# A longer list of first operations for local attention and channel mix on one core, with split products that follow it

## The chip, the cores and the metric

The kernel runs on one core of a Trainium2 chip. The core has a matrix engine (TensorE, PE in the profile), three engines for element-wise work (VectorE or DVE, ScalarE or ACT, GpSimd or POOL) and SyncE (SP), whose queue issues all the kernel's DMAs. The metric is the device time of one execution in microseconds; smaller is better.

## The reference

Two layers stand one behind the other. The first is chunked local attention on 4 batches, 8 heads, 768 tokens and 64 features a head; each chunk of 32 queries sees 16 keys to its left, its own 32, 8 to its right and 8 memory keys. The second is a channel mix over 512 features and 1024 hidden ones.

```python
for c in range(nc):                       # 24 chunks of 32 queries
    k_full = concat([mem_k, k[l_start:r_end]])
    v_full = concat([mem_v, v[l_start:r_end]])
    scores = scale * q_c @ k_full.T
    a = exp(scores - max(scores)); a = a / (sum(a) + 1e-9)
    out[c_start:c_end] = a @ v_full
...
x = out as (batch, token, 512)
x_prev = x shifted by one token, zeros first
xk = mu_k * x + (1 - mu_k) * x_prev
xr = mu_r * x + (1 - mu_r) * x_prev
v = maximum(xk @ w_k, 0) ** 2 @ w_v
return sigmoid(xr @ w_r) * v
```

The weights and mu come as 64-bit floats.

## The kernel before

The 3072 tokens are cut into 24 tiles of 128 (index t) and 12 units of two tiles (index u). The work is a list of some 770 named operations, each with a cost, the engines that may run it, its dependencies, and the buffers it takes and uses. The names are those of the prediction:

- **Weights.** There are ten chunks of 1 MiB: w0 and w1 hold w_r, w2 to w5 hold w_k, w6 to w9 hold w_v. Each is loaded as 64-bit words (`w4.load`) and turned into a pair of fp32r tiles by five steps: `mag` (ScalarE) and `low` (VectorE) take the word apart, `join` (VectorE) puts a 32-bit float together, `hi` rounds it (ScalarE or VectorE), and `lo` is the rest (VectorE or GpSimd).
- **Attention.** `qk` and `vw` are a tile's loads. For each unit `s` makes the scores on TensorE, `max` and `sub` (VectorE) and `exp` (ScalarE) the softmax, `sum` (one reduction and two small steps) and `norm` finish it. For each tile `t` transposes on TensorE, `bd.0` and `bd.1` copy the result into a block-diagonal tile, `a` multiplies with the values, and `x` copies the result into the unit's xT. For the first tile of a unit, `x` also copies one column from the unit before, always on ScalarE.
- **Mix.** `df` is the difference to the shifted tokens, `mix.1` and `mix.0` the two blends, and `xh` and `xl` their high and low halves. `mix.1`, `xh.1`, `xl.1` feed the gate and `mix.0`, `xh.0`, `xl.0` the hidden layer.
- **Products.** A product of two pairs is three fp32r products. `g` is the gate (tile pr, 128x512 matmuls), `h` the hidden layer (tile ph, 128x256 matmuls), `v` the output (tile pv, 128x512). `relu`, `sq`, `kh` and `kl` turn a hidden bank into a pair, `sig` is the gate's sigmoid, `o` multiplies, and `out` stores. In unit 0, `h0.n` takes one w_k chunk (w2 + n) for all four hidden banks, so that it can begin before all chunks are there; `g0.n` and `v0.n` do the same with w_r and w_v. `g0.0` needs w0, h0.0 needs w2. In later units `h` and `g` are one bank each.

Buffers tie the loads to the work. Weight words and qk tiles share four buffers (`big`), vw has three. SyncE's queue goes in order, and a load waits there until the buffer's last reader is done.

The order is fixed in Python before anything is issued. `Plan.order` first places the items of the string FIRST, in that order, each on the engine written behind the @. What is left it places by itself, always the operation that can start first by the plan's costs; the order of TensorE alone then follows due times made from `te_order`. Each engine runs its own operations in the order in which they were placed; only semaphores tie the engines together. Between TensorE's operations ahead of h0.0 the kernel puts warm-up matmuls on zeros wherever the plan sees a gap. Each of these is two instructions in the trace.

`product` can write its 512 columns in two matmuls of 256. Before, that is so for the last product of `g` in the second tile of each unit and of `v` in the second tile of unit 1.

Of the kernel before, what the change touches and what calls it, by code (L numbers as in the profile page):

```python
# [16 lines left out]
P = 128  # L17
# [7 lines left out]
KT = DM // P  # L25
# [7 lines left out]
QPU = UTOK // P  # L33
# [5 lines left out]
TABLE = 1.3  # L39
BLOCK = 2.75  # L40
FIRST = """
w4.load@dma w4.low@dve qk1@dma w4.mag@act w4.join@dve w4.hi@dve w4.lo@dve qk0@dma s0@pe max0@dve sub0@dve
w3.load@dma w3.mag@act w3.low@dve w3.join@dve exp0@act sum0@dve norm0@dve qk3@dma w3.hi@act w3.lo@pool qk2@dma
s1@pe max1@dve id@dma t0@pe bd0.0@act bd0.1@act mu@dma t1@pe sub1@dve w2.load@dma w2.low@dve w2.mag@act
w2.join@dve exp1@act sum1@dve bd1.1@act vw1@dma bd1.0@act vw0@dma a0@pe a1@pe x0@act x1@act norm1@dve t2@pe
bd2.1@act bd2.0@act qk5@dma df0@dve mix0.1@dve mix0.0@dve w5.load@dma w5.mag@act w2.hi@act w2.lo@dve vw2@dma
qk4@dma s2@pe max2@dve xh0.0@act xl0.0@pool t3@pe bd3.1@act sub2@dve vw3@dma bd3.0@act w1.load@dma w1.mag@act
a2@pe a3@pe w5.low@dve w5.join@dve w5.hi@act w0.load@dma w0.mag@act w1.low@dve w1.join@dve w0.low@dve
w0.join@dve qk6@dma w5.lo@dve exp2@act sum2@dve norm2@dve w0.hi@act w0.lo@dve xh0.1@act xl0.1@dve x2@act
x3@act df1@dve w1.hi@act w1.lo@dve h0.0@pe h0.1@pe h0.2@pe h0.3@pe relu0.1@act sq0.1@act relu0.0@act kh0.1@dve  # L50
kl0.1@dve sq0.0@act kh0.0@act t4@pe bd4.1@act bd4.0@act t5@pe bd5.0@act bd5.1@act qk7@dma s3@pe max3@dve
g0.0@pe g0.1@pe mix1.1@dve xh1.1@dve xl1.1@dve vw4@dma a4@pe kl0.0@dve w7.load@dma w7.low@dve w7.mag@act
mix1.0@dve xh1.0@dve xl1.0@dve w6.load@dma w6.mag@act w6.low@dve vw5@dma a5@pe relu0.2@act sq0.2@act
relu0.3@act sq0.3@act kh0.3@act w7.join@dve w7.hi@dve sig0.0@act sig0.1@act kh0.2@act vw6@dma w8.load@dma
w8.mag@act g1.0@pe sig1.0@act w7.lo@dve w6.join@dve w6.hi@dve w6.lo@dve g1.1@pe sig1.1@act kl0.3@dve vw7@dma
kl0.2@dve h1.0@pe h1.1@pe h1.2@pe h1.3@pe relu1.0@dve sq1.0@act qk9@dma x4@act x5@act sub3@dve exp3@act
relu1.1@dve
"""
PE_COST = {"s": 1.4, "t": 0.45, "a": 1.05, "g": BLOCK, "h": BLOCK, "v": BLOCK}
BIAS = {"act": 0.0, "dve": 0.3, "pool": 0.3}  # L60
# [22 lines left out]
class Plan:  # L83
# [123 lines left out]
def local_attention__then__channel_mix(  # L207
# [31 lines left out]
    def ps(tag, name, n=1):  # L239
        return psA.tile([P, n * 512], F32, tag=tag, name=name, bufs=bufs[tag])  # L240
# [22 lines left out]
    plan = Plan(bufs)  # L263
# [9 lines left out]
    def either(**alts):  # L273
        return [(n, *alts[n]) for n in alts]
# [60 lines left out]
    def wdeps(hl, ks):  # L335
        return [o for k in ks for o in wdone[id(hl[0]), k]]
# [181 lines left out]
    def channel_mix(u):  # L518
        b, t0 = units[u]

        def hilo(m):
            return T["xh", u, m], T["xl", u, m]

        def product(p, x, w, start, stop, halves):
            step = DM // 2 if halves else DM
            for a in range(0, DM, step):
                nc.tensor.matmul(  # L527
                    p[:, a : a + step], x, w[:, a : a + step], start=start, stop=stop and a + step == DM
                )

        def gate(c, ks):
            p = T["pr", u, c]
            xh, xl = hilo(1)
            for k in ks:
                wh, wl = (w[k // 2][:, k % 2 * DM : (k % 2 + 1) * DM] for w in wr_hl)
                for n, (x, w) in enumerate(((xh, wh), (xh, wl), (xl, wh))):
                    stop = k == KT - 1 and n == 2
                    product(p, x[:, k, c * P : (c + 1) * P], w, k + n == 0, stop, stop and c == QPU - 1)

        def hidden(f, ks):  # L540
            p = T["ph", u, f]
# [8 lines left out]
                        stop = k == KT - 1 and n == 2 and (u > 0 or i == 1)  # L550
                        nc.tensor.matmul(z, w, x[:, k], start=start, stop=stop)  # L551
# [18 lines left out]
        first = u == 0  # L570
# [42 lines left out]
        for n in range(FT // 2):  # L613
# [10 lines left out]
            w = wdeps(wk_hl, [n] if first else range(KT))  # L624
# [8 lines left out]
        ks = []  # L633
        for f in range(FT // 2):
# [28 lines left out]
            o2 = op(f"kh{u}.{f}", either(act=(0.6,), dve=(0.36, True)), f_hi, [ob], new=[kh], use=[kf])  # L663
# [49 lines left out]
    for u in range(NU):  # L713
        channel_mix(u)
    engines = {"act": nc.scalar, "dve": nc.vector, "pool": nc.gpsimd}
    warm = None
    zero = zero_sb.bitcast(F32)
    zeros = zero.unsqueeze(1).to_broadcast([P, 4, P])
    busy = 0.0
    with tc.manual_schedule():  # L720
        for o in plan.order(FIRST.split()):
            if o.eng == "pe":
                n = 0 if ("ph", 0, 0) in T else int((o.start - busy - 0.1) / (0.86 if busy else 1.72))
                for _ in range(n):
                    warm = warm or ps("m", "warm")
                    nc.tensor.matmul(warm, zero, zeros, start=True, stop=True)  # L726
# [50 lines left out]
```

## Time and profile before

| | |
|---|---|
| median of 3 runs | 418.64 us (417.03 to 419.3) |
| the profiled execution, its own time | 414.7 us |
| its span, first to last instruction | 412.9 us |
| TensorE busy | 402.4 us, 97% of the span |
| VectorE, ScalarE, GpSimd busy | 247.0, 193.5 and 17.7 us |
| read from HBM, written | 42.01 MB, 6.29 MB |

The views name an instruction by its line, its engine, the operation and what it writes and reads (out<-in), without buffer numbers. In the timeline the first number is the start and the second the length, in us from the span's start; what ended the engine's idle time stands in brackets. In the groups by line the numbers after the bar are the busy time, the mean length of one in ns, and the idle time ahead. A busy TensorE isn't one at its peak, since its instructions overlap and their ends are modelled. VectorE is 92% to 100% busy between 40 and 90 us; from 90 us on the kernel repeats one unit's work about every 32 us.

### The profile page before, as it was taken

To read this page: it belongs to the slowest core of one execution; us is meant where nothing else is said; L and a number is where in the kernel's file an instruction comes from. 1 tells how busy PE (TensorE), PEld (TensorE's weight loads), DVE (VectorE), ACT (ScalarE), POOL (GpSimd) and SP (SyncE) were. 2 spreads that over 40 slices of the span, in tenths; PEclk is the share of its full clock that TensorE was granted. 3 is DMA by queue.
4 is the path that set the end of the run, shared out by engine and by line. 5 is a ranking of instruction groups with operands and counts; after the bars stand their busy time and mean duration, and the time that the engine had idled before them with its cause. 6 is when DMAs were issued, how large, how long until landed. Compare 5 with 4: busy or idle time off the path is not lost.

```text
span 412.9 us, 9915 instructions
## 1 busy us (share of the span) xinstructions
PE 402.4 (97%) x4463; PEld 349.7 (85%) x4463; DVE 247.0 (60%) x356; ACT 193.5 (47%) x275; POOL 17.7 (4%) x20
## 2 busy tenths in 40 slices
PE   7789999999999999999999999999999999999996
PEld 3448989888988988988988988988988998998994
DVE  3999999981286287178169169169259348337021
ACT  2376964840633634543553453463363264363250
POOL 2202000010000010010010010010010010010000
PEclk9999999999999999999999999999999999999999
DMA  8998966211261062062053043034003002000001
GB/s 324 375 415 313 397 210 223 76 51 52 78 249 59 0 233 79 0 214 94 2 193 115 2 160 148 2 144 139 27 2 129 25 3 78 25 2 27 25 2 51
DMA packets 12906, 48.94 MB, mean 119 GB/s; under 512 B 1472, under 2 KB 1600, under 8 KB 12352
## 3 DMA queue, kind: packets, MB, share of 16 engines
q1 hardware_dynamic: 12864, 48.31, 32.0%
q8 instruction: 35, 0.57, 0.6%
q14 instruction: 7, 0.06, 0.0%
HBM read 42.01 MB, written 6.29 MB: 117 GB/s over the span
## 4 chain that ended last, share of the span: by engine, by line
PE 92%; DMA 5%; DVE 2%; SPq 0%; issue 0%; DVEq 0%
PE pv L527 33%; PE ph L551 32%; PE pr L527 16%; PE px L444 5%; DMA qk<-in_qk_dram 5%; PE s L365 4%; PE pt L427 2%; DVE mx L378 0%; DVE mag L318 0%; DVE e L382 0%; DVE sum L394 0%; PE warm L726 0%; SPq L295 0%; DVE o L696 0%; DVE raw L314 0%
## 5 line engine op out<-in xcount | busy, mean ns | idle before, releaser
L551 PE MATMUL ph<-xh,wkh 128*128 128x256 f32 x384 | 106.2, 277 | 0.0
L551 PE MATMUL ph<-xl,wkh 128*128 128x256 f32 x384 | 106.1, 276 | 0.0
L551 PE MATMUL ph<-xh,wkl 128*128 128x256 f32 x384 | 106.0, 276 | 0.0
L655 DVE TENSOR_TENSOR kl<-kf,kh 128x512 fp32r<-128x512 f32 x47 | 32.3, 690 | 112.3 <-ACT kh L269 112.2
L527 PE MATMUL pv<-wvh,kh 128*128 128x512 f32 x192 | 76.8, 400 | 0.0
L527 PE MATMUL pv<-wvh,kl 128*128 128x512 f32 (+1 forms) x193 | 75.0, 389 | 0.0
L527 PE MATMUL pv<-wvl,kh 128*128 128x512 f32 x192 | 74.8, 390 | 0.0
L551 PEld LDWEIGHTS ph<-xh,wkh 128*128 128x128 f32 x384 | 72.1, 188 | 0.1
L551 PEld LDWEIGHTS ph<-xl,wkh 128*128 128x128 f32 x384 | 72.1, 188 | 0.0
L551 PEld LDWEIGHTS ph<-xh,wkl 128*128 128x128 f32 x384 | 72.1, 188 | 0.0
L638 ACT ACTIVATE kf<-ph 128x512 f32<-128x512 f32 x46 | 27.5, 599 | 56.8 <-PE ph L551 53.0
L527 PEld LDWEIGHTS pv<-wvh,kh 128*128 128x128 f32 x192 | 36.0, 188 | 8.2
L527 PEld LDWEIGHTS pv<-wvh,kl 128*128 128x128 f32 x193 | 36.2, 188 | 7.8
L527 PEld LDWEIGHTS pv<-wvl,kh 128*128 128x128 f32 x192 | 36.1, 188 | 6.9
L527 PE MATMUL pr<-wrh,xh 128*128 128x512 f32 x96 | 37.6, 391 | 0.0
L527 PE MATMUL pr<-wrh,xl 128*128 128x512 f32 (+1 forms) x108 | 37.5, 365 | 0.0
L527 PE MATMUL pr<-wrl,xh 128*128 128x512 f32 x96 | 37.4, 389 | 0.0
L598 ACT ACTIVATE sg<-pr 128x512 f32<-128x512 f32 x24 | 14.1, 598 | 47.8 <-PE pr L527 47.7
L269 ACT CAST kh<-kf 128x512 fp32r<-128x512 f32 x46 | 28.5, 620 | 4.2 <-POOL kf L647 2.4
L444 PEld LDWEIGHTS px<-aTz,vw 128*64 128x64 f32 x768 | 23.6, 138 | 7.0 <-issue 5.7
L269 ACT CAST xh<-xf 128x1024 fp32r<-128x1024 f32 x11 | 11.6, 1053 | 38.0 <-DVE xf L500 38.0
L645 ACT ACTIVATE kf<-kf 128x512 f32<-128x512 f32 x38 | 24.0, 632 | 7.2 <-DVE kf L640 6.0
(62 smaller groups left out, 498.9 us busy)
## 6 DMA issues: line engine op xcount, KB each, us to landing
qk<-in_qk_dram SPq DMA_DIRECT2D x24, 768.0 KB, 5.9
vw<-in_vw_dram SPq DMA_DIRECT2D x24, 512.0 KB, 5.5
out_dram<-o SPq DMA_DIRECT2D x24, 256.0 KB, 2.0
raw<-in_w_k_dram SPq DMA_DIRECT2D x4, 1024.0 KB, 8.7
raw<-in_w_v_dram SPq DMA_DIRECT2D x4, 1024.0 KB, 7.3
raw<-in_w_r_dram SPq DMA_DIRECT2D x2, 1024.0 KB, 7.8
id_sb<-in_ident_dram SPq DMA_DIRECT2D x1, 64.0 KB, 6.4
mu_sb<-in_mu_dram SPq DMA_DIRECT2D x1, 4.0 KB, 6.1
```

The costliest lines, as they stand in the source:

```text
L269: e.copy(dst, src)
L365: nc.tensor.matmul(s5[CHUNK * j : CHUNK * (j + 1), h, c, r, :], q4[z, r, j, :], k4[z, r, j, :], start=True, stop=True,)
L427: nc.tensor.transpose(p[:, n * P : (n + 1) * P], e[:, n // 2, c, n % 2, :], id_sb)
L444: nc.tensor.matmul(p3[64 * h : 64 * h + 64, 2 * g : 2 * g + 2, CHUNK * j : CHUNK * j + CHUNK], v[:, g, h, j, :], a[:, h, g, j, :], start=True,
L527: nc.tensor.matmul(p[:, a : a + step], x, w[:, a : a + step], start=start, stop=stop and a + step == DM)
L551: nc.tensor.matmul(z, w, x[:, k], start=start, stop=stop)
L598: nc.scalar.activation(T["sg", u][:, c * DM : (c + 1) * DM], T["pr", u, c], AF.Sigmoid)
L638: e.activation(r, T["ph", u, f], AF.Relu)
L645: e.activation(q, q, AF.Square)
L655: e.tensor_sub(l, T["kf", u, f], T["kh", u, f].bitcast(F32))
```

## The change

FIRST grows from 170 to 273 items, and all are new in order: it now reaches up to unit 2's output products (v2.3), where the old list ended in unit 1's hidden layer. The weight chunks come in another order (w5, w2, w3, w4, w0, w1, w7, w6, w9, w8 in place of w4, w3, w2, w5, w1, w0, w7, w6, w8, w9). On TensorE h0.0 has the same eleven operations ahead of it as before, and behind it the first units are arranged anew; from h3.0 on the order is that of before. Where the first output product v0.0 came behind all of unit 1's hidden products, it now comes ahead of h1.3.

The second part: which last products are written in two matmuls is no longer fixed by tile and unit. The kernel looks through TensorE's order for each `h` that directly follows a `g` or `v`, and marks the latter.

```diff
-w4.load@dma w4.low@dve qk1@dma w4.mag@act w4.join@dve w4.hi@dve w4.lo@dve qk0@dma s0@pe max0@dve sub0@dve
...
+w5.load@dma w5.mag@act w5.low@dve w5.join@dve w5.hi@act w5.lo@dve qk0@dma qk1@dma s0@pe max0@dve id@dma w2.load@dma
...
-        def gate(c, ks):
+        def gate(c, ks, kick):
...
-                    product(p, x[:, k, c * P : (c + 1) * P], w, k + n == 0, stop, stop and c == QPU - 1)
+                    product(p, x[:, k, c * P : (c + 1) * P], w, k + n == 0, stop, stop and c in kick)
...
-        def value(c, fs):
+        def value(c, fs, kick):
...
-                        product(p, x[:, tc_], w, f + n == 0, stop, stop and c == QPU - 1 and u == 1)
+                        product(p, x[:, tc_], w, f + n == 0, stop, stop and c in kick)
...
-                        gate(c, range(n * KT // 2, (n + 1) * KT // 2))
+                        gate(c, range(n * KT // 2, (n + 1) * KT // 2), ())
...
-                    gate(n, range(KT))
+                    gate(n, range(KT), [n] if ("g", u, n) in kicks else ())
...
-                    value(c, fs)
+                    value(c, fs, [QPU - 1 if first else c] if ("v", u, n) in kicks else ())
...
+    done = plan.order(FIRST.split())
+    te = [o.name for o in done if o.eng == "pe"]
+    kicks = set()
+    for a, b in zip(te, te[1:]):
+        if b[0] == "h" and a[0] in "gv":
+            kicks.add((a[0], *map(int, a[1:].split("."))))
...
-        for o in plan.order(FIRST.split()):
+        for o in done:
```

ScalarE, from the copy of a1's result to what follows xh0.0, before. The names end in a number that the program gives each tile; mag5 is chunk w5, aTz0 and aTz1 are the block-diagonal tiles, wkh0 is w2's high half, xh0_0 the hidden layer's high half of unit 0.

```order
L269 COPY xT0_344<-px1_327 128x4x128
L269 COPY aTz0_86<-pt2_350 64x16x32 x2
L311 ACTIVATE mag5_372<-raw5_370 128x1024
L269 CAST wkh0_66<-mag2_294 128x1024
L269 CAST xh0_0_450<-df0_359 128x1024
L269 COPY aTz1_87<-pt3_454 64x16x32 x2
```

The same stretch of ScalarE after:

```order
L276 CAST wkh1_67<-mag3_203 128x1024
L318 ACTIVATE mag4_433<-raw4_431 128x1024
L276 COPY aTz0_86<-pt2_420 64x16x32 x2
L276 COPY aTz1_87<-pt3_440 64x16x32 x2
L465 COPY xT1_473<-xT0_324 128x4
L276 COPY xT1_473<-px2_456 128x4x128
L276 CAST xh0_0_494<-df0_350 128x1024
L276 COPY xT1_473<-px3_476 128x4x128
L276 CAST wkh2_68<-mag4_433 128x1024
L276 CAST xh0_1_609<-xf0_425 128x1024
```

Both tiles' copies (bd) and x2 (the two rows that write xT1) have moved ahead of xh0.0, w4.mag stands ahead of them, and w4.hi and the gate's xh0.1 follow closely.

VectorE between sub2 and norm2 before (norm2 is the last row; wkl3 is w5's low half):

```order
L382 TENSOR_TENSOR e2_460<-s2_382,mx2_448 128x1024
L314 TENSOR_SCALAR raw5_370<-raw5_370 128x1024
L318 SCALAR_TENSOR_TENSOR mag5_372<-mag5_372,raw5_370 128x1024
L314 TENSOR_SCALAR raw1_465<-raw1_465 128x1024
L318 SCALAR_TENSOR_TENSOR mag1_467<-mag1_467,raw1_465 128x1024
L314 TENSOR_SCALAR raw0_507<-raw0_507 128x1024
L318 SCALAR_TENSOR_TENSOR mag0_509<-mag0_509,raw0_507 128x1024
L324 TENSOR_TENSOR wkl3_73<-mag5_372,wkh3_69 128x1024
L394 TENSOR_REDUCE sum2_519<-e2_460 128x16
L395 TENSOR_SCALAR sum2_519<-sum2_519 128x16
L396 RECIPROCAL sum2_519<-sum2_519 128x16
L400 TENSOR_TENSOR e2_460<-e2_460,sum2_519 128x1024
```

VectorE from xl0.0 on after (wkl1 and wkl2 are the low halves of w3 and w4, wrl0 and wrl1 of w0 and w1); sum2's two small steps and norm2 come next:

```order
L517 TENSOR_TENSOR xl0_0_496<-df0_350,xh0_0_494 128x1024
L321 TENSOR_SCALAR raw0_452<-raw0_452 128x1024
L331 TENSOR_TENSOR wkl1_71<-mag3_203,wkh1_67 128x1024
L331 TENSOR_TENSOR wkl2_72<-mag4_433,wkh2_68 128x1024
L383 MEMSET s2_352 32x2x4x8
L385 TENSOR_REDUCE mx2_614<-s2_352 128x16
L389 TENSOR_TENSOR e2_620<-s2_352,mx2_614 128x1024
L325 SCALAR_TENSOR_TENSOR mag0_611<-mag0_611,raw0_452 128x1024
L321 TENSOR_SCALAR raw1_616<-raw1_616 128x1024
L325 SCALAR_TENSOR_TENSOR mag1_618<-mag1_618,raw1_616 128x1024
L331 TENSOR_TENSOR wrl0_84<-mag0_611,wrh0_82 128x1024
L331 TENSOR_TENSOR wrl1_85<-mag1_618,wrh1_83 128x1024
```

xl0.0, which was GpSimd's, is VectorE's now, and four low halves stand ahead of norm2 in place of one.

GpSimd's first element-wise operations after (before they were w3's low half, xl0.0, one kl of unit 1, and then one square in each unit):

```order
L331 TENSOR_TENSOR wkl0_70<-mag2_185,wkh0_66 128x1024
L517 TENSOR_TENSOR xl0_1_624<-xf0_425,xh0_1_609 128x1024
L662 TENSOR_TENSOR kl0_1_758<-kf0_1_635,kh0_1_729 128x512
L662 TENSOR_TENSOR kl0_0_768<-kf0_0_637,kh0_0_732 128x512
L662 TENSOR_TENSOR kl0_2_1023<-kf0_2_816,kh0_2_917 128x512
L662 TENSOR_TENSOR kl0_3_1070<-kf0_3_901,kh0_3_961 128x512
L662 TENSOR_TENSOR kl1_2_1224<-kf1_2_1211,kh1_2_1216 128x512
L662 TENSOR_TENSOR kl2_1_1404<-kf2_1_1309,kh2_1_1399 128x512
```

On TensorE, h0.0 to h0.3, t4, t5, s3, g0.0, g0.1, a4, a5, g1.0 before has become h0.0 to h0.3, s3, g0.0, t4, t5, g0.1, a4, a5, s4, g1.0.

More of the change, by code (lines that the diff above doesn't have):

```diff
@@ L41 @@
 FIRST = """
-w4.load@dma w4.low@dve qk1@dma w4.mag@act w4.join@dve w4.hi@dve w4.lo@dve qk0@dma s0@pe max0@dve sub0@dve
[L43 to L56, printed above, removed]
@@ L57 @@
-relu1.1@dve
+w5.load@dma w5.mag@act w5.low@dve w5.join@dve w5.hi@act w5.lo@dve qk0@dma qk1@dma s0@pe max0@dve id@dma w2.load@dma
+w2.mag@act w2.low@dve qk3@dma qk2@dma sub0@dve w2.join@dve exp0@act w2.hi@act sum0@dve w3.load@dma w3.mag@act vw0@dma
+s1@pe norm0@dve t0@pe t1@pe w3.low@dve w2.lo@pool qk4@dma bd0.1@act bd0.0@act bd1.0@act a0@pe bd1.1@act vw1@dma
+max1@dve sub1@dve qk5@dma exp1@act x0@act w3.join@dve sum1@dve a1@pe x1@act df0@dve s2@pe norm1@dve mu@dma t2@pe
+mix0.1@dve w3.hi@act w4.load@dma w4.mag@act vw2@dma w4.low@dve bd2.0@act bd2.1@act t3@pe bd3.1@act vw3@dma mix0.0@dve
@@ new lines @@
+w0.load@dma bd3.0@act a2@pe x2@act a3@pe w4.join@dve xh0.0@act xl0.0@dve h0.0@pe w0.low@dve w3.lo@dve x3@act h0.1@pe
+w4.hi@act w4.lo@dve vw4@dma vw5@dma h0.2@pe h0.3@pe xh0.1@act w0.mag@act max2@dve w1.load@dma w1.mag@act sub2@dve
+qk7@dma xl0.1@pool w0.join@dve exp2@act w1.low@dve w1.join@dve w0.hi@act w0.lo@dve vw6@dma w1.hi@act relu0.1@act
+relu0.0@act qk6@dma sq0.0@act s3@pe g0.0@pe qk9@dma w1.lo@dve sum2@dve sq0.1@act kh0.1@act norm2@dve kh0.0@act
+w7.load@dma w7.mag@act t4@pe t5@pe bd4.0@act bd4.1@act qk8@dma df1@dve bd5.0@act max3@dve kl0.1@pool mix1.1@dve
@@ new lines @@
+sub3@dve bd5.1@act kl0.0@pool g0.1@pe a4@pe a5@pe relu0.2@act xh1.1@act s4@pe sq0.2@act xl1.1@dve g1.0@pe relu0.3@act
+exp3@act mix1.0@dve sq0.3@act x4@act x5@act sum3@dve kh0.2@dve xh1.0@act g1.1@pe w6.load@dma w6.mag@act norm3@dve
+t6@pe t7@pe xl1.0@dve w6.low@dve w7.low@dve w7.join@dve sig0.0@act vw7@dma sig0.1@act vw8@dma kh0.3@act bd6.1@act
+h1.0@pe h1.1@pe w9.load@dma max4@dve sub4@dve sig1.0@act sig1.1@act kl0.2@pool bd6.0@act a6@pe h1.2@pe bd7.1@act
+bd7.0@act kl0.3@pool w6.join@dve relu1.0@act sq1.0@act w6.hi@dve w8.load@dma a7@pe w9.mag@act w8.mag@act w9.low@dve
@@ new lines @@
+w7.hi@act w8.low@dve w6.lo@dve w9.join@dve relu1.1@act v0.0@pe h1.3@pe w9.hi@act w8.join@dve x6@act sq1.1@act qk13@dma
+vw9@dma w7.lo@dve df2@dve w8.hi@act w8.lo@dve x7@act qk10@dma qk11@dma v0.1@pe v0.2@pe mix2.1@dve mix2.0@dve w9.lo@dve
+vw10@dma kh1.0@act exp4@act kl1.0@dve xh2.0@act xl2.0@dve relu1.2@act sq1.2@act kh1.1@dve kh1.2@act kl1.1@dve
+relu1.3@act qk12@dma kl1.2@pool v0.3@pe o0.1@dve h2.0@pe o0.0@dve h2.1@pe out0.1@dma sq1.3@dve xh2.1@act kh1.3@dve
+kl1.3@dve relu2.0@act xl2.1@dve sq2.0@dve out0.0@dma df3@dve relu2.1@act mix3.1@dve mix3.0@dve v1.0@pe v1.1@pe v1.2@pe
@@ L58 @@
+sq2.1@act v1.3@pe o1.0@dve h2.2@pe kh2.1@dve o1.1@dve out1.1@dma kl2.1@pool kh2.0@act kl2.0@dve relu2.2@dve sq2.2@act
+h2.3@pe relu2.3@act kh2.2@dve sq2.3@act kl2.2@dve out1.0@dma g2.0@pe sig2.0@act g2.1@pe xh3.1@act kh2.3@dve v2.0@pe
+kl2.3@dve v2.1@pe v2.2@pe o2.0@dve sig2.1@act v2.3@pe
 """
```

## The prediction

> **What bounds the kernel now.** I read the page first, its busy times (the share of the span in brackets):
>
> ```profile
> PE 402.4 (97%) x4463; PEld 349.7 (85%) x4463; DVE 247.0 (60%) x356; ACT 193.5 (47%) x275; POOL 17.7 (4%) x20
> ```
>
> TensorE is the bound. The chain of waits in order of time (start, length, what) says where it still has room:
>
> ```profile
> 1.64 7.77 DMA qk<-in_qk_dram
> ...
> 18.82 11.87 DMA qk<-in_qk_dram
> ...
> 36.02 11.10 PE ph L551 x96
> 47.11 0.87 PE pt L427 x8
> 47.99 1.41 PE s L365 x89
> 49.40 5.69 PE pr L527 x25
> 55.08 2.02 PE px L444 x64
> 57.10 5.67 PE pr L527 x25
> 62.77 10.90 PE ph L551 x96
> ...
> 409.09 0.69 DVE o L696
> ```
>
> From 36.02 (h0.0, behind a3) to 409.09 every piece is TensorE's own work, one behind the other. That work (373.07 us) is the same in both kernels, and so are the 3.8 us behind it. So the time can change in two ways only: **h0.0 starts at another moment than 36.0, or TensorE waits behind it**. A new order cannot gain more than it takes off those 36 us, and both lists put the same eleven items (s0 to s2, t0 to t3, a0 to a3) ahead of h0.0.
>
> **Front: when can h0.0 start?** These are the timeline rows of ScalarE, TensorE, VectorE and GpSimd there (start, length):
>
> ```profile
> 17.32 3.00 DVE L400 TENSOR_TENSOR e<-e,sum 128x1024 f32<-128x1024 f32 x1
> 25.49 0.20 ACT L456 COPY xT<-zero_sb 128x4 f32<-128x4 f32 x1
> 25.59 0.58 ACT L269 COPY xT<-px 128x512 f32<-128x512 f32 x1
> 25.69 1.15 PE L444 MATMUL px<-aTz,vw 128*64 128x64 f32 x32
> 26.88 0.59 ACT L269 COPY xT<-px 128x512 f32<-128x512 f32 x1 [0.71 <-PE px L444]
> 27.75 0.63 PE L427 MATMUL pt<-id_sb,e 128*128 128x128 f32 x4
> 28.21 1.88 PE L726 MATMUL warm<-zero_sb 128*128 128x512 f32 x4
> 28.47 1.17 ACT L269 COPY aTz<-pt 64x512 f32<-64x512 f32 x2 [1.01 <-PE pt L427]
> 29.55 1.14 ACT L311 ACTIVATE mag<-raw 128x1024 f32<-128x1024 f32 x1
> 30.36 1.67 DVE L500 SCALAR_TENSOR_TENSOR df<-df,mu_sb,xT 128x256 f32<-128x256 f32 x4
> 32.06 1.05 ACT L269 CAST xh<-df 128x1024 fp32r<-128x1024 f32 x1 [0.43 <-DVE df L500]
> 33.18 2.40 POOL L510 TENSOR_TENSOR xl<-df,xh 128x1024 fp32r<-128x1024 f32 x1 [13.95 <-ACT xh L269]
> ```
>
> Before, mix0.0 ends at 32.03, xh0.0 follows at once and xl0.0 takes 2.40 us on GpSimd, to 35.58. After, xl0.0 is VectorE's: the like-sized L324 takes 1.22 (row below), 1.2 saved. But xh0.0 now stands on ScalarE behind w4.mag, bd2.0 to bd3.0 and x2, hence behind a2. VectorE reaches mix0.0 no earlier: norm0 ends some 0.3 sooner than 20.32, and one more "low" (0.69) stands ahead of mix0.0, so it ends near 32.3. norm1 ends near 28.2 (20.0 plus low, max, sub, join, sum, df, norm, 8.5 us, less 0.1 for each overlap), t2 follows, and the first copy comes 0.72 behind t2 (27.75 to 28.47): 29.0.
>
> ScalarE runs w4.mag ahead of these copies, so **the landing of w4 decides**. Ahead of and with w4 the new queue has four weight chunks of 1 MiB, six qk of 0.75 and two vw of 0.5: 9.5 MiB. The second qk lands at 1.64 + 7.77 = 9.41 with 2.5 MiB done, in both orders, leaving 7.0 MiB. Two rates can be had:
>
> ```profile
> 20.00:30.00 10.00, 8.47 (x86) 4.88 (x86) 9.65 (x14) 7.13 (x12) 0.00 (x0) 1.00 1.02 417
> ```
>
> At 417 GB/s (2.51 us a MiB) w4 lands at 27.0. But qk4 landed at 18.82 + 11.87 = 30.69 with 10 MiB done, 7.5 MiB in 21.28 us or 2.84 a MiB, and by that w4 lands at 29.3. Late end: w4.mag to 30.45, two copies (1.17) to 31.65, a2, x2 1.19 later (25.69 to 26.88) to 33.55, xh0.0 to 34.6, xl0.0 to 35.85, h0.0 at 35.9. TensorE's own side says the same: a3 at 32.85, then four warm-up matmuls (1.88) up to 35.85. Early end: copies from 29.0, a2 at 30.25, x2 to 32.1, xh0.0 from 32.3, h0.0 at 34.65. The gain on the front is so 0.1 to 1.3 us. I take 0.4, nearer the late end, whose rate was measured over the same stretch.
>
> **Behind h0.0: the wait at t4.** Before, norm2 ended at 45.7 and t4 ran at 47.11, after the four hidden products. After, s3 and g0.0 come first, so t4 is due 11.10 + 1.41 + 5.69 / 2 = 15.4 us behind h0.0's start, and norm2 needs more of VectorE than before, since w3.lo, w4.lo and both w_r chunks' joins and lows now stand ahead of it. The durations:
>
> ```profile
> L314 DVE TENSOR_SCALAR raw<-raw 128x1024 uint32<-128x1024 uint32 x10 | 6.9, 689 | 4.7 <-DMA raw<-in_w_k_dram 4.7
> L318 DVE SCALAR_TENSOR_TENSOR mag<-mag,raw 128x1024 uint32<-128x1024 uint32 x10 | 12.2, 1223 | 1.0 <-ACT mag L311 0.5
> L324 DVE TENSOR_TENSOR wkl<-mag,wkh 128x1024 fp32r<-128x1024 f32 x3 | 3.7, 1221 | 0.0
> L378 DVE TENSOR_REDUCE mx<-s 128x16 f32<-128x1024 f32 x12 | 14.7, 1224 | 0.4
> L382 DVE TENSOR_TENSOR e<-s,mx 128x1024 f32<-128x1024 f32 x12 | 14.6, 1219 | 0.2
> L394 DVE TENSOR_REDUCE sum<-e 128x16 f32<-128x1024 f32 x12 | 14.5, 1210 | 0.0
> 44.48 1.23 DVE L400 TENSOR_TENSOR e<-e,sum 128x1024 f32<-128x1024 f32 x1
> 45.62 1.22 DVE L324 TENSOR_TENSOR wrl<-mag,wrh 128x1024 fp32r<-128x1024 f32 x1
> ```
>
> From xl0.0's end: two lows 1.38, two joins 2.45, four lo 4.88, max2 with its memset 1.4, sub2 1.2, sum2 with two small steps 1.7, norm2 1.23: 14.2 us, less 0.09 for each of some seven that start before the one ahead has ended (44.48 + 1.23 against 45.62), 13.6 us. That would be 1.8 ahead of need. What undoes it is GpSimd:
>
> ```profile
> 16.89 2.35 POOL L324 TENSOR_TENSOR wkl<-mag,wkh 128x1024 fp32r<-128x1024 f32 x1 [13.94 <-ACT wkh L269]
> L655 POOL TENSOR_TENSOR kl<-kf,kh 128x512 fp32r<-128x512 f32 x1 | 1.3, 1293 | 52.3 <-ACT kh L269 52.3
> ```
>
> While the first ran, norm0 took 3.00 instead of 1.23: it ended 1.08 after GpSimd had done (19.24, 20.32). So a VectorE operation on two SBUF tiles stands still until GpSimd is through. The new order gives GpSimd xl0.1 when xh0.1 is done: ScalarE's x3 (0.59), w4.hi and xh0.1 (1.05 each) follow xh0.0, which ends 1.25 ahead of h0.0, so 1.4 behind h0.0. That falls inside w3.lo, and w4.lo is next on VectorE. If GpSimd (2.4 us) comes in ahead of it, w4.lo ends near 4.9 instead of 3.0 behind h0.0: 1.9 lost, and the cover is gone. Then norm2 is ready at about 14.3, just as GpSimd gets kl0.1 (five ScalarE steps on 512 columns, 0.58 each like x0's copy or a little more, behind the hidden products' end at 11.1: 14.0 to 14.4): another 1.29 or nothing. If nothing, df1 stands still instead, and sub3 gates s4: behind norm2 come df1, max3, mix1.1 and sub3 (5.2 us of VectorE) against t4, t5, g0.1, a4, a5 (5.6 of TensorE), so the wait only moves to s4 and shrinks by 0.4. **I take 1.3 us; the bounds are 0 (GpSimd never first) and 2.7 (kl0.0 follows kl0.1 at once, another 1.3).**
>
> The Trainium skill, "SBUF — State Buffer", section "Who interferes with whom", speaks against this change: GpSimd and VectorE share a port pair, the one that issues first holds it for its whole instruction, and a VectorE operation with two SBUF inputs is blocked by a GpSimd operation that reads SBUF. The trace agrees (norm0, 3.00). By that rule the sum is +0.9; without it, -0.4.
>
> **The rest.** Split products: eleven instead of thirteen last products are halved.
>
> ```profile
> 62.15 0.39 PE L527 MATMUL pr<-wrl,xh 128*128 128x512 f32 x1
> 62.38 0.40 PE L527 MATMUL pr<-wrh,xl 128*128 128x256 f32 x2
> L551 PEld LDWEIGHTS ph<-xh,wkh 128*128 128x128 f32 x384 | 72.1, 188 | 0.1
> ```
>
> Two halves took 0.40 together, one whole 0.39: nothing. But v0.0 to h1.3 is now a boundary from 512 to 256 columns without a split, which before never has. If hidden products then ran at the load's 188 ns instead of 114 (10.90 / 96), 24 of them would cost 1.8; below, nothing is to be had. I take 0: h0.0 behind a3 has no split either and pays 0.2 in all. Later moves cost nothing: v0.0, the first to need w_v, still has unit 1's gate and most of its hidden layer ahead of it, some 40 us of TensorE behind h0.0's start, and now s4 and t6 to a7 too; from h3.0 on TensorE's order is that of before.
>
> **Sum**, against the profiled execution (span 412.9, its own time 414.7): -0.4 + 1.3 + 0 = **+0.9, span 413.8**. The median of the runs shown, 418.64, lies 3.9 above that execution; the change is added to it: 419.5.
>
> **Rivals.**
> - *VectorE keeps its port* (30%): w4.lo issues before GpSimd's xl0.1, norm2 is done 1.8 ahead of need, nothing waits at t4, only the front's gain is left: 418.2, down to 417.3 with w4 landing early. For: it follows w3.lo without a gap. Against: in the one case of the trace GpSimd was first. The skill's rule in that section, that who issues first wins, allows both.
> - *GpSimd takes it twice* (15%): kl0.0 goes directly behind kl0.1 while norm2 stands; wait 2.6, front 0.1: 421.1, slower. It decides if kh0.0 is done before kl0.1's 1.29 us are over, which it should be as ScalarE's next step, and if the waiting VectorE doesn't come between.
> - *The split does not act where it is needed* (7%): v0.0 isn't the last step of its sum, so the flag set for it halves nothing; with 1.8 on top of the forecast: 421.3.
> - *The front gains more than its early end* (3%): the whole 1.3 and more, with no wait behind: 416.5 or less.
> - Forecast, the wait eats the front's gain (45%): 419.5, by itself 418.4 to 420.5.
>
> **How the numbers follow.** All but the two slower rivals and the last one stay within 0.5% (2.1 us, about what a measurement can tell from no change). Faster by more needs the last rival: 0.05. Slower by more: both slower rivals lie at +2.5 and +2.7, some of them below the bound: 0.18. The rest, 0.77, is within. The range goes from the early end with no wait (417.3), less half a microsecond for the runs' own spread (417.03 to 419.3), to the slow rivals (421.3) with the same: 416.8 to 421.8.
>
> **What would show it.** In the chain of waits: h0.0's first ph piece at 35.5 (34.65 to 35.9), behind xl0.0 on VectorE. A w4.lo of some 3 us beside GpSimd's xl0.1, norm2 stretched beside kl0.1, and a VectorE piece of 1 to 1.5 us between pr and pt at about 51. If w4.lo and norm2 both take 1.22, the rival holds. h1.3's 24 matmuls should take 2.73, 4.5 if the split matters. I am wrong if h0.0 starts before 34.5, or if a wait of over 0.5 us stands behind s4.

## The result, and the profile after

| | before | after |
|---|---|---|
| median (four runs each) | 418.40 us (417.03 to 419.30) | 422.90 us (422.67 to 423.12) |
| span of the profiled execution | 412.9 us | 421.1 us |
| first hidden product h0.0 starts | 35.95 us | 40.31 us |
| from there to the end of the span | 377.0 us | 380.8 us |

The ratio after to before is 1.011, with a 95% interval of 1.0082 to 1.0139: slower by some 4.5 us, and above the predicted range, which ended at 421.8. The page of after gives TensorE 404.5 us of busy time and before 402.4, nearly the same. The time went into pauses and into a slower clock. First the head of the page, TensorE's busy share and its granted clock, in 40 slices of 10.5 us, the clock in tenths:

```profile
span 421.1 us, 9904 instructions
PE   8749989999999999999999999999999999999996
PEclk9997999999999999999999999999999999999999
```

The third slice of PE and the fourth of PEclk stand out: around 26 to 37 us TensorE pauses, and then runs at a lower clock. The chain of waits of after (start, length, what) names the pieces there:

```profile
25.48 1.49 PE s L372 x104
26.96 4.57 issue
31.54 0.43 PE s L372 x4
31.96 2.00 PE warm L739 x2
33.97 1.71 PE pt L434 x8
```

"issue" is time in which the engine waited for nothing that the profile shows. It lies in the middle of s2: 124 of its 128 small matmuls run in 1.56 us, TensorE stands for 4.57 us, and four more follow. No load, no buffer and no other engine is named. Then two warm-up matmuls and the eight transposes t2 and t3 take 2.00 and 1.71 us; four and eight took 1.88 and 0.87 in before's profile. The windows of after say why (PE busy, PEld, DVE, ACT, POOL, then the granted clock, the DMA share and GB/s):

```profile
28.00:30.00 2.00, 0.00 (x0) 0.00 (x0) 2.00 (x6) 1.14 (x1) 0.00 (x0) 0.89 1.03 408
34.00:36.00 2.00, 2.00 (x9) 1.80 (x8) 0.00 (x0) 1.07 (x3) 0.00 (x0) 0.50 0.08 23
```

The clock is at a half from 30 to 36 us. By the mean of 0.89 between 28 and 30 us it fell at about 29.6 (0.44 us at a half), some 2.6 us into the pause. The Trainium skill, "TensorE: Matmul & The Clock Gate", section "What's actually happening", has the clock at half after at least one idle window of about 3.4 us. Here it fell sooner, and the measurement decides.

Behind h0.0, the two waits in which VectorE and GpSimd meet. Timeline rows of VectorE and GpSimd, and the two rows of TensorE that waited (in brackets the idle time and what ended it):

```profile
41.38 4.56 DVE L331 TENSOR_TENSOR wkl<-mag,wkh 128x1024 fp32r<-128x1024 f32 x2
42.06 2.79 POOL L517 TENSOR_TENSOR xl<-xf,xh 128x1024 fp32r<-128x1024 f32 x1 [23.46 <-ACT xh L276]
55.78 3.51 POOL L662 TENSOR_TENSOR kl<-kf,kh 128x512 fp32r<-128x512 f32 x2 [10.92 <-ACT kh L276]
55.80 2.34 DVE L407 TENSOR_TENSOR e<-e,sum 128x1024 f32<-128x1024 f32 x1
58.06 2.31 DVE L499 TENSOR_TENSOR df<-xT 128x1024 f32<-128x1024 f32 x1
58.19 1.09 PE L434 MATMUL pt<-id_sb,e 128*128 128x128 f32 x8 [1.75 <-DVE e L407]
64.64 1.74 PE L372 MATMUL s<-qk 64*32 64x64 f32 x128 [0.58 <-DVE e L389]
```

w3.lo and w4.lo (the first row) take 4.56 us together where 2.4 were worked out; norm2 (e<-e,sum) 2.34 and df1 2.31 where 1.2 each. Each time a GpSimd operation is in flight: xl0.1 started 0.45 ahead of w4.lo (42.51 in the records), kl0.1 0.02 us ahead of norm2. TensorE pays at t4 (1.75) and, through df1 and sub3, at s4 (0.58).

### The profile page after: what moved, and what is told of

It is laid out like the page before. It is cut to its first block, busy times and chain, and to the rows that moved or that the text cites. A ratio compares the mean times of both kernels' runs of the same rounds, so it can differ in the third digit from the quotient of the medians.

```text
span 421.1 us, 9904 instructions
## 1 busy us (share of the span) xinstructions
PE 404.5 (96%) x4459; PEld 351.1 (83%) x4459; DVE 244.8 (58%) x345; ACT 194.5 (46%) x278; POOL 30.2 (7%) x26
## 4 chain that ended last, share of the span: by engine, by line
PE 87%; DVE 5%; DMA 4%; issue 2%; SPq 1%; ACT 0%; DVEq 0%
PE pv L534 32%; PE ph L558 29%; PE pr L534 15%; PE px L451 5%; PE s L372 3%; PE pt L434 3%; DMA raw<-in_w_k_dram 2%; DMA vw<-in_vw_dram 2%; DVE wkl L331 1%; DVE mag L325 1%; PE warm L739 1%; DVE e L407 1%; DVE wrl L331 1%; DVE raw L321 0%; DVE e L389 0%
## 5 line engine op out<-in xcount | busy, mean ns | idle before, releaser
L662 DVE TENSOR_TENSOR kl<-kf,kh 128x512 fp32r<-128x512 f32 x42 | 29.0, 691 | 106.4 <-ACT kh L276 106.2
L703 DVE TENSOR_TENSOR o<-pv,sg 128x512 f32<-128x512 f32 x24 | 16.0, 671 | 23.9 <-PE pv L534 23.9
L276 ACT CAST kh<-kf 128x512 fp32r<-128x512 f32 x42 | 26.0, 621 | 8.4 <-PE pv L534 5.3
L276 ACT CAST xh<-xf 128x1024 fp32r<-128x1024 f32 x12 | 12.6, 1053 | 36.8 <-DVE xf L507 34.9
```

Of the source, the lines that this page charges most:

```text
L276: e.copy(dst, src)
L662: e.tensor_sub(l, T["kf", u, f], T["kh", u, f].bitcast(F32))
L703: nc.vector.tensor_mul(o, T["pv", u, c], T["sg", u][:, c * DM : (c + 1) * DM])
```

## What TensorE waits for in s2

The page of after has a line for a DMA queue that no operation of the kernel issues:

```profile
q8 instruction: 35, 0.57, 0.6%
```

These are 35 packets, 16 KB each. The trace has 8970 records on TensorE (matmuls, weight loads, semaphore events); 8970 / 35 is 256.3 for each packet. Reading the packets as blocks of TensorE's program gives a theory: **TensorE runs dry of instructions.** A block of 256 is fetched while the block ahead is worked through. One s is 256 instructions (128 matmuls, each with its weight load) in 1.4 us. If the next block takes longer than that to come, TensorE stands, wherever in the program the border lies, and nothing that the kernel says is waited for.

To test that, TensorE's records are numbered from 0 in order of their starts. The table holds every pause of over 0.6 us that the profile puts to "issue" and that stands in front of one of the numbers 193 + 256 k, for all kernels of this study (those below included), and beside it the packet of the queue that came last before TensorE went on:

| kernel | number | pause (start to start) | packet | from the packet's end to going on |
|---|---|---|---|---|
| before, 1st profile | 961 | none (reached at 31.82) | 29.26 to 30.33 | - |
| before, 2nd | 961 | 31.48 to 33.89 | 31.37 to 32.40 | 1.49 |
| before, 3rd | 961 | 32.37 to 34.01 | 31.60 to 32.63 | 1.38 |
| after | 961 | 26.75 to 31.54 | 29.07 to 30.10 | 1.44 |
| fill16 | 961 | 26.33 to 30.33 | 27.86 to 28.90 | 1.43 |
| fill48 | 705 | 18.34 to 24.20 | 21.60 to 22.67 | 1.53 |
| fill48 | 961 | 31.83 to 32.95 | 30.61 to 31.57 | 1.38 |
| fill48 | 1217 | 37.57 to 39.17 | 36.73 to 37.75 | 1.42 |
| fill48 | 2241 | 69.64 to 70.91 | 68.36 to 69.42 | 1.49 |
| oldsplit | 961 | 26.62 to 30.86 | 28.45 to 29.52 | 1.34 |
| oldsplit | 1985 | 64.41 to 65.11 | 62.14 to 63.46 | 1.65 |
| s2late | 961 | 33.57 to 35.36 | 32.88 to 33.94 | 1.42 |
| s2behind | 1985 | 59.71 to 60.82 | 58.19 to 59.39 | 1.43 |
| s2behind_port | 1985 | 58.43 to 59.65 | 56.97 to 58.18 | 1.47 |
| s2behind_port_xl | 1217 | 40.96 to 41.99 | 39.67 to 40.58 | 1.41 |
| s2behind_port_xl | 1985 | 59.81 to 60.75 | 58.17 to 59.29 | 1.46 |
| port | 961 | 26.88 to 31.11 | 28.55 to 29.62 | 1.49 |
| port | 1985 | 62.01 to 63.75 | 61.05 to 62.36 | 1.39 |
| s2late_port_s4 | 961 | 33.62 to 34.54 | 32.15 to 33.25 | 1.29 |
| s2late_port_s4 | 1217 | 40.43 to 42.11 | 39.71 to 40.62 | 1.49 |

The pauses fall into scores, attention products, hidden products and the gate's products alike, and TensorE goes on 1.3 to 1.7 us behind a packet's end. Of all the pauses over 0.6 us that the profile puts to "issue" in these traces, only two stand elsewhere, both at number 652 ahead of a1 (1.19 us in before's third profile, 0.83 in b_s2late). By this it is the late block that bounds s2. The experiments ask whether the pauses move as this says, and what they and the waits behind h0.0 cost.

## The experiments

**The kernel before again (b_again, b_third).** No edit; a second and a third profile.

> The kernel before, unchanged, profiled once more. The kernel before was timed at 417.0 to 419.3, but its one profiled execution took 414.7; the kernel after takes 422.7 to 423.1 both ways. Theory 'instructions' (TensorE ran dry of instructions inside s2 in the changed kernel, as its block of instructions came late): in the kernel before the same block arrives only some 0.3 us before it is needed, so in other executions it may come too late, s2 is then cut as well, and spans spread between 412.9 and some 417, with a granted clock under 0.999 where the stop is long. Rival 'own wait' (s2 in the changed kernel waits for one of its own operands): the kernel before has no such stop in any execution; spans all near 413 and the rest of the timed median has another cause outside the span.

> The kernel before, unchanged, for a third profile. In the first (span 412.9) h0.0 began at 35.95, in the second (416.5) at 39.50: from h0.0 to the end both took 377.0. Theory 'the spread of its times is the stop at the 961st instruction': the span less the start of h0.0 is again 376.8 to 377.2, and the pause at that instruction accounts for the rest: under 0.5 us of pause for a span up to 413.5, 1.5 to 3 us for 415.5 to 417.5. Rival 'the spread comes from elsewhere, a load that lands late or the clock': a span over 415.5 without such a pause, or a rest that is not 377.0.

Measured: 418.03 us (ten runs, 416.81 to 419.29) and 418.60 (seven, 416.64 to 419.38); profiled spans 416.5 and 415.1. The chain of waits of the second profile, and then of the third:

```profile
30.34 1.35 PE s L365 x81
31.69 2.20 issue
33.89 0.35 PE s L365 x16
```

```profile
32.59 1.42 issue
34.01 0.35 PE s L365 x16
```

Both have the pause, at the same number, and the first profile, on which the prediction was built, has none: there the packet ended 1.49 us ahead of number 961, just in time. From h0.0 to the end all three take 377.0 us (412.9 - 35.95, 416.5 - 39.50, 415.1 - 38.09): all of the spread of these three spans lies ahead of h0.0. In the second, the clock shows 0.50 behind a pause of 2.2 us; the row of the windows, as above:

```profile
36.00:38.00 2.00, 2.00 (x17) 1.07 (x14) 1.97 (x3) 1.16 (x2) 0.00 (x0) 0.50 0.84 325
```

In the third, behind 1.42 us, it stayed at 1.00. The Trainium skill, "TensorE: Matmul & The Clock Gate", section "What's actually happening", gives an idle window of about 3.4 us for that; a pause of 2.2 us was enough here. So most of the spread of these three executions is whether, and how long, TensorE runs dry in s2. One part of the third span is not: its a1 came late as well (26.89), behind 1.19 us of "issue", at number 652, which is no border; what that was is open.

**Moving the border (fill16, fill48).** 16 or 48 small matmuls on zeros ahead of s1, which add 64 or 192 TensorE instructions.

```diff
+                if o.name == "s1":
+                    for k in range(FILL):
+                        j = k % NJ
+                        nc.tensor.matmul(
+                            warm[CHUNK * j : CHUNK * (j + 1), :NK], zero[:64, :CHUNK], zero[:64, :NK],
+                            start=True, stop=True,
+                        )
```

> The same with 16 tiny matmuls (64 instructions). Theory 'instructions': the border comes 64 instructions earlier in s2, and the request 64 earlier too, which is some 2 us earlier as it falls ahead of a1, that waits for its vw; the stop in s2 shrinks to about 3 us (2.4 to 3.5) and begins about 0.35 us sooner within s2 (after 92 of its 128 matmul records instead of 124). Rival 'own wait': 4 to 5 us at the same place, after 124.

> The changed kernel with 48 more tiny matmuls on zeros (192 more instructions of TensorE) ahead of s1, where TensorE stands idle for 3 us. Theory 'instructions': each block is 256 instructions, is asked for when TensorE enters the one ahead of it and can be used some 6.2 us later; 192 more instructions ahead put the block's border that now cuts s2 before s2's first quarter and its request at the end of s1, so the stop of 4.6 us inside s2 goes, the clock stays at full speed, and h0.0 starts 4 to 5 us sooner (at 35.5 to 36.3 instead of 40.3). Span 415.5 to 417 instead of 421.1. Rival 'own wait': more work ahead of s1 takes nothing away; the stop in s2 stays at 4 to 5 us, span 421 or a little more.

fill16: one run, 421.81 us. The pause came 64 records earlier within s2 (behind 92 matmuls in place of 124) and at the same number 961, as expected; it lasted 3.78 us and not the 2.4 to 3.5 expected. Its chain of waits:

```profile
25.45 1.10 PE s L373 x81
26.55 3.78 issue
30.33 0.87 PE s L373 x36
```

fill48: 425.86 us, ratio to before 1.0193 (1.0157 to 1.0229), slower than after and not faster. Its chain of waits has four pauses, none of them at the place where after has its one: 0.88 us at 70.03, amid the gate's products, and ahead of it these three:

```profile
17.27 1.29 PE s L373 x75
18.56 5.64 issue
...
32.05 0.91 issue
...
37.79 1.38 issue
```

The pause moved by the count, as the theory has it, and the time was expected wrong: with 192 instructions more, TensorE got through the block up to number 705 in one rush (the added matmuls and s1), and ran dry there for 5.64 us. A border that is shifted away from one burst falls into another. That the pause belongs to s2's operands, as a rival would have it, is out: the same s2 is cut at another matmul, and s1 is cut as well.

**s2 elsewhere (s2late, s2behind).** In the changed kernel s2 follows a1 and s1 closely. In s2late it stands behind a3, in s2behind behind h0.0; the other engines keep their order.

```diff
-max1@dve sub1@dve ... a1@pe x1@act df0@dve s2@pe norm1@dve mu@dma t2@pe
+max1@dve sub1@dve ... a1@pe x1@act df0@dve norm1@dve mu@dma t2@pe
...
-w0.load@dma bd3.0@act a2@pe x2@act a3@pe w4.join@dve xh0.0@act ...
+w0.load@dma bd3.0@act a2@pe x2@act a3@pe s2@pe w4.join@dve xh0.0@act ...
```

> The changed kernel with one item of its list moved: s2 behind a3 instead of behind a1. Theory 'instructions': the block asked for at about 25.3 is there at 31.5, before s2 starts at 32.5 to 33.5, so nothing stops; h0.0 at 35.5 to 36.5, span 415.5 to 417. Rival 'own wait' (qk4, qk5 or the scores' bank come late): no stop either, as all of it is there by then, so this run does not tell the two apart; it shows what the stop costs in all. If the stop is instead tied to s2's 256 instructions whatever stands ahead, a gap of 4 us stays inside s2 and the span stays at 421.

> The changed kernel with s2 on TensorE moved from behind a1 to behind h0.0 (its first 24 matmuls of the hidden layer); all else in the same order. Theory 'TensorE runs dry at its 961st instruction, since it gets through 256 of them in less time than the next block takes to come': in the kernel with s2 behind a3, the block's packet ended at 33.94 and TensorE went on at 35.36. Here only short instructions up to a3 and h0.0 (48 instructions in 2.7 us) stand ahead of s2, so the 961st comes at about 38 us, when the block is there: no stop of over 0.7 us within s2, h0.0 starts at 34.4 to 35.2 (xl0.0 ends at 34.96 there), s2 runs in 1.4 to 1.5 us at about 37.7; median 414.8 to 416.2. Rival 's2 stops wherever it is put, for its qk loads or a buffer': a stop of 1.5 us or more within s2 behind h0.0, 416.5 to 418.

s2late: 416.95 us (ten runs, 416.65 to 417.40), ratio to before 0.9984 (0.9972 to 0.9996). One TensorE operation moved takes 6 us off after's 422.90. Its timeline still shows a pause in s2, of 1.57 us, where none was expected, and the clock stays up behind it; h0.0 starts at 36.37, though s2 now stands directly ahead of it, against 40.31:

```profile
33.11 0.68 PE L372 MATMUL s<-qk 64*32 64x64 f32 x43
35.36 1.07 PE L372 MATMUL s<-qk 64*32 64x64 f32 x85 [1.57 <-issue]
36.37 0.38 PE L558 MATMUL ph<-xh,wkh 128*128 128x256 f32 x1
```

The start of h0.0 shows 3.9 of the 6 us; xl0.0 on VectorE shows them all. It started 5.89 us earlier than in after (33.74, 39.63), VectorE took the same 18.5 us from there to norm2's end, GpSimd's holds included, and t4, which waits for norm2 in both, started 5.94 us earlier (52.25, 58.19).

s2behind: 417.31 us (416.90 to 418.49), ratio 0.9982 (0.9958 to 1.0006). As expected, there is no pause in s2 (1.48 us in one piece at 37.81; the block's packet had ended at 33.68), and h0.0 starts at 34.51. The time expected, 414.8 to 416.2, did not come. The chain of waits says what took it:

```profile
40.12 8.45 DMA qk<-in_qk_dram
...
48.71 1.47 PE s L372 x85
...
59.93 0.90 issue
```

s3 waits for the load of its queries and keys. Weight words and qk tiles share four buffers, s2 reads two of them, and a later s2 frees them later. Behind that, s4 runs dry at number 1985. The rival's number (416.5 to 418) fits, its reason does not.

**GpSimd off VectorE's back (port).** xl0.1, kl0.1 and kl0.0 on VectorE.

```diff
-qk7@dma xl0.1@pool w0.join@dve ...
+qk7@dma xl0.1@dve w0.join@dve ...
...
-... max3@dve kl0.1@pool mix1.1@dve
-sub3@dve bd5.1@act kl0.0@pool g0.1@pe ...
+... max3@dve mix1.1@dve
+sub3@dve bd5.1@act kl0.1@dve kl0.0@dve g0.1@pe ...
```

> The changed kernel with three operations moved from GpSimd to VectorE: xl0.1 (at the same place of the list), kl0.1 and kl0.0 (both behind sub3). VectorE gets 1.22 + 2 x 0.69 = 2.6 us more work. Theory 'GpSimd holds up VectorE behind h0.0': w4.lo takes 1.22 instead of 3.43, norm2 1.23 instead of 2.34, df1 1.15 instead of 2.31; norm2 ends 1.9 to 2.1 earlier against h0.0, the wait ahead of t4 (2.13 us from instruction to instruction) falls to 0.3 or less, that ahead of s4 (0.80) stays or falls to 0.2; median 420.2 to 421.2, against 422.9 for the changed kernel. The stop within s2 (4.79) stays as it is. Rival 'VectorE is behind by its own work, whoever does xl0.1': the wait at t4 stays at 2 us or grows, 422.5 to 424.

421.76 us (six runs, 420.61 to 423.36), ratio to before 1.0090 (1.0059 to 1.0121); that of after was 1.0110 with an interval that overlaps, so the gain in time is not told apart, and the 420.2 to 421.2 expected did not come. The rows tell the cause all the same. The first three are VectorE's (w3.lo with w4.lo, norm2, df1), the others TensorE's chain:

```profile
40.32 2.35 DVE L331 TENSOR_TENSOR wkl<-mag,wkh 128x1024 fp32r<-128x1024 f32 x2
53.69 1.23 DVE L407 TENSOR_TENSOR e<-e,sum 128x1024 f32<-128x1024 f32 x1
54.83 1.22 DVE L499 TENSOR_TENSOR df<-xT 128x1024 f32<-128x1024 f32 x1
```

```profile
52.32 2.95 PE pr L534 x12
55.27 0.87 PE pt L434 x8
...
61.01 1.21 PE s L372 x76
62.22 1.52 issue
```

With these operations off GpSimd, each takes its 1.2 us, and the waits at t4 and s4 are gone, though VectorE has 2.5 us more to do: both were GpSimd's doing. But TensorE, earlier at s4, reaches number 1985 before its block and stands for 1.52 us. From h0.0 on 380.0 us remain, of after's 380.8 (spans less the start of h0.0, 39.26).

**Both, and on (s2behind_port, s2behind_port_xl, s2late_port_s4).** The edits together; then w4.join behind xl0.0 on VectorE, which xl0.0 need not wait for; or s2 behind a3 with s4 behind g1.0, so that number 1985 comes later.

```diff
-... a3@pe w4.join@dve xh0.0@act xl0.0@dve h0.0@pe s2@pe ...
+... a3@pe xh0.0@act xl0.0@dve w4.join@dve h0.0@pe s2@pe ...
```

```diff
-... xh1.1@act s4@pe sq0.2@act xl1.1@dve g1.0@pe ...
+... xh1.1@act sq0.2@act xl1.1@dve g1.0@pe s4@pe ...
```

> Both edits together: s2 behind h0.0, and xl0.1, kl0.1, kl0.0 on VectorE. If the two causes are apart, the gains add: the one with s2 behind h0.0 less what is left of the waits at t4 and s4 there (0.5 to 1.5 us): 413.8 to 415.2. If VectorE's extra 2.6 us of work costs as much as GpSimd's hold, the same as with s2 behind h0.0 alone, within 0.4 us.

> The same with w4.join moved on VectorE from ahead of xl0.0 to behind it. Theory: xl0.0 is what h0.0's second matmul waits for now, and w4.join (1.22 us) stands ahead of it, so h0.0's products begin 0.8 to 1.2 us earlier, while w4 is not needed before h0.2, 6.9 us later: 0.5 to 1.2 us less than without this move. Rival: h0.0 waits for xh0.0 or for a3 and its warm-up matmuls, or the later w4.hi comes back as a wait at h0.2 or t4: within 0.3 us.

> The changed kernel with s2 behind a3 (416.95 in the run of that alone), with xl0.1, kl0.1 and kl0.0 on VectorE, and with s4 behind g1.0 instead of ahead of it. In the run with the three operations on VectorE the 1985th instruction, which lies in s4, came too early for its block (1.74 us). With g1.0's 24 long matmuls ahead of s4 that border is reached some 5.6 us later: no stop over 0.4 us there. Theory 'only the stops and the waits at t4 and s4 are left': 415.2 to 416.3. Rival 'VectorE is the bound from 60 to 75 us, and what TensorE gains up to s4 it waits for at h1.0 (xl1.0) and a6': within 0.5 of 416.95.

Measured: 417.59 us, ratio 0.9985 (0.9966 to 1.0005); 418.33, ratio 1.0005 (0.9985 to 1.0025); 416.81, ratio 0.9966 (0.9949 to 0.9984). None reached what its theory expected. The first came within 0.4 us of s2behind alone, as its rival had it: its chain of waits runs over VectorE for nearly all the way from max2 (39.34) to xl1.0, whose end at 66.89 releases h1.0, so VectorE is the bound there. The second took 0.7 us more than the first, where 0.5 to 1.2 less or, by its rival, the same within 0.3 was expected. The last has the lowest median here, not told apart from s2late's 416.95. Its rival's number (within 0.5 of 416.95) fits and its reason does not: h1.0 and a6 wait for nothing. There is no wait left at t4 or s4 and no pause in s4; its chain of waits has instead

```profile
33.83 0.71 issue
34.54 1.07 PE s L372 x64
35.61 5.09 PE ph L558 x43
40.70 1.41 issue
```

a pause amid the hidden products. From number 961 to 1217 lie the rest of s2 and 43 hidden matmuls, 1.07 + 5.09 = 6.2 us; the packet ended 7.4 us behind the one before it. Each wait taken away so far brought another one forward. In this stretch (34 to 42 us) the DMA share is 0.76 to 0.99, and instructions come more slowly than they are used. s2behind_port's own profile has its pause at number 1985 only; the one with w4.join moved has both.

**The split alone undone (oldsplit).** The new order with the old rule for products in two parts.

```diff
-    kicks = set()
+    kicks = {("g", u, 1) for u in range(1, NU)} | {("v", 1, 1)}
...
-        if b[0] == "h" and a[0] in "gv":
-            kicks.add((a[0], *map(int, a[1:].split("."))))
+        pass
```

> The changed kernel with its new order, but split products chosen by the old rule (the last product of g in the second tile of each unit, of v in the second tile of unit 1): the second part of the change is undone alone. Theory 'the split costs and brings nothing': the median of the changed kernel, 422.9, within 0.6. Rival 'the split rule has a share in the 4.5 us': 420 to 422, or over 423.6.

422.57 us (four runs, 422.42 to 423.33), ratio 1.0107 (1.0080 to 1.0135), beside after's 1.0110: the second part of the change costs and brings nothing that can be measured. h1.3 behind an unsplit v0.0 takes 2.83 us in both (after's chain of waits):

```profile
86.48 2.83 PE ph L558 x24
```

**The kernel before with s2 moved (b_s2late).** The same remedy on the old order; max2 and sub2 moved on VectorE so that it does not wait for s2.

```diff
-qk4@dma s2@pe max2@dve xh0.0@act xl0.0@pool t3@pe bd3.1@act sub2@dve vw3@dma ...
+qk4@dma xh0.0@act xl0.0@pool t3@pe bd3.1@act vw3@dma ...
-a2@pe a3@pe w5.low@dve ...
+a2@pe a3@pe s2@pe w5.low@dve ...
-w0.join@dve qk6@dma w5.lo@dve ...
+w0.join@dve max2@dve sub2@dve qk6@dma w5.lo@dve ...
```

> The kernel before, with s2 on TensorE moved behind a3, and max2 and sub2 on VectorE moved behind w0.join, so that VectorE does not stand waiting for it. In the second profile of the kernel before, TensorE stood 2.42 us within s2 and ran at half clock behind it, and h0.0 began at 39.50; without such a stop it began at 35.95. Theory 'the same stop is in most executions of the kernel before': s2 is now directly ahead of h0.0, which begins at 36.8 to 38.2, and the spread of the times shrinks: median 414.8 to 417.0. Rival 'what s2 gains it loses behind h0.0': norm2 comes 6.7 us of VectorE behind s2 at the earliest, and the loads of qk6 and qk7 wait for s2's buffers: a wait of over 1.5 us ahead of t4 or s3, median 417.5 to 419.5.

420.64 us (419.64 to 423.62), ratio 1.0071 (1.0040 to 1.0101): the theory's 414.8 to 417.0 is out. The rival was right that what s2 gains is lost behind h0.0, and wrong in the place (t4 or s3) and in the size (417.5 to 419.5). h0.0 started at 36.88, without a pause in s2, but the chain of waits behind it reads

```profile
37.18 4.90 DMA raw<-in_w_r_dram
...
47.32 1.14 DVE wkl L324
...
48.51 5.07 PE ph L551 x22
```

The load of w0 began only behind s2 (which ended at 36.9), with whose tiles it shares the four buffers, and w5.lo, which the last hidden product waits for, stood on VectorE behind max2, sub2 and w0's join. TensorE idled 2.96 us for it, and the clock was at 0.50 behind that, from 48 to 54 us: the 22 matmuls took 5.07 us, where 2.5 are usual (0.114 each).

## Why the prediction was wrong, point by point

**The front (-0.4 predicted).** Against the profiled execution h0.0 came 4.36 us later, against the second and third profiles of before 0.8 and 2.2 later. The step that failed is the one that worked out h0.0's start from loads, copies and engines alone, and let s2 pass without a cost of its own. The loads and copies were right: w4 landed at 28.66 (27.0 to 29.3 predicted), norm1 ended at 28.5 (28.2), w4.mag at 29.82, so that the copies could have begun there. They began at 34.92, since t2 stood behind s2 on TensorE and ran at the half clock. 5.1 us earlier h0.0 would have been at 35.2 (an estimate), within the predicted 34.65 to 35.9. What the new order does worse is that s2 follows a1 directly: TensorE got from number 705 to 961 in 1.6 us (25.14 to 26.75) and needed a block that lands at 30.10. Before's s2 started only at 30.73, and in its first profile the same way took 5.4 us (26.44 to 31.82).

**The base (418.64 as 3.9 above the profiled execution).** The prediction took that distance for an offset and added the change to it. In the two further profiles it was mostly the pause: of three executions of before, the one without it was the one predicted from. Counted against the other two, after's 4.6 or 6.0 us are 0.8 or 2.2 ahead of h0.0 and 3.8 behind it. This does not separate the causes, since in after t4 waits for VectorE's work, which begins with the late xl0.0: s2late, which leaves GpSimd's operations as they are, is no slower than before (0.9984).

**Behind h0.0 (+1.3 predicted, bounds 0 and 2.7).** The mechanism was right, its size too small: the term of 1.3 measured about 2.5, and 1.3 more had no term. 380.8 against 377.0 makes +3.8: some 1.9 at t4 (1.75 of idling) and 0.6 at s4, together 2.5 by GpSimd's hold; 0.4 at h0.0's second matmul, which xl0.0 keeps waiting for 0.60 in place of 0.22 us; the rest, about 0.9, is spread over s4 and the products up to a7. The prediction had the wait either at t4 or at s4. It came at both: kl0.1 held norm2, GpSimd's kl0.0 then waited for norm2 and held df1 next (the rows above). The rule of the Trainium skill that the prediction weighed ("SBUF — State Buffer", "Who interferes with whom") held: kl0.1 was issued 0.02 us ahead of norm2, and norm2 stood.

**The rest (0 predicted).** True: oldsplit, and 2.83 for h1.3. Later moves cost nothing: the v products of unit 0 wait for no load.

**The rivals.** "VectorE keeps its port" fell (w4.lo 3.43, norm2 2.34). "GpSimd takes it twice" was nearest in its 2.6 us, but in another way: norm2 waited for one kl only. "The split does not act" had its condition come true, since v0.0 ends in one matmul of 512 columns, but not its price: h1.3 took 2.83 and not 4.5. None of them held the cause of the front's loss, which the view of before could have raised in one row: s, 128 matmuls in 1.48 us, a queue named "instruction", and a distance of 3.9 us to the median that no term explained.

What stays open: what sets the time from when TensorE enters a block to when the next one's packet comes. In after that was 3.9 us (25.14, number 705, to 29.07), in s2late 8.0 (24.87 to 32.88). Both fall into stretches with the DMA share at about 1.0, and no kernel here lowered that load with all else kept; that the loads' traffic sets it is argued, not shown. What the late xl0.0 and GpSimd's holds each cost in after is not separated either: no run has the one without the other and no new pause.

## What to carry to other kernels

On a program that is unrolled into thousands of instructions, count instructions beside time: bursts of short ones (256 in 1.4 us) outran their own fetching here, in a stretch in which loads filled the DMA queues, and such a burst is best kept away from the one before and where its end is not waited for. Compare a change with several profiles of the kernel before: a single one may be an execution that missed a pause which most have. Ahead of giving GpSimd a two-input operation, ask what VectorE does at that moment, and count the time on both engines.

## What the runs showed of the hardware that was not expected

- TensorE pauses at borders 256 instructions apart (seen at 705, 961, 1217, 1985 and 2241) when the packet of the queue "instruction" has not come; it goes on 1.3 to 1.7 us behind the packet's end. Pauses of 0.7 to 5.6 us were seen, and the profile calls them "issue".
- The granted clock fell to 0.50 with pauses at a border of 2.20 us (before's second profile) and more, and stayed at 1.00 behind 1.42 us (its third). The length alone does not decide: ahead of s1 TensorE idled 2.67 us in s2behind and the clock stayed at 1.00, and 2.38 us in s2late, where it fell to 0.50 (18 to 20 us).
- An operation on 128x16 elements was held up as long as a large one: in s2late the first small step of a sum ran beside GpSimd's w2.lo for 2.36 us, while the same step takes 0.17 elsewhere. The rows of VectorE and GpSimd:

```profile
16.24 2.35 POOL L331 TENSOR_TENSOR wkl<-mag,wkh 128x1024 fp32r<-128x1024 f32 x1 [13.30 <-ACT wkh L276]
16.26 2.36 DVE L402 TENSOR_SCALAR sum<-sum 128x16 f32<-128x16 f32 x1
```
